# A fused attention and gated feed-forward kernel: the first combine spread over engines, one reciprocal moved to VectorE, two loads and stage 1 in later slots

## The chip, the core and the metric

The kernel runs on one core of a Trainium2 chip. A core has five engines with queues of their own: TensorE (PE; its weight loads are listed apart as PEld), VectorE (DVE), ScalarE (ACT), GpSimd (POOL) and SyncE (SP, which here only issues DMAs). Each engine works through its queue in order and waits on semaphores for the others. DMAs are issued from POOL (loads that cast from float32 to float16) and from SP (stores, and DMAs that transpose). The metric is the device time of one execution in microseconds (us).

## The reference

```python
def _attn_ref(x, inducing):            # x: 4 x 12416 x 128, inducing: 32 x 128
    def mab(q, kv):
        s = scale * (q @ kv.transpose(0, 2, 1))
        s = s - s.max(-1, keepdims=True)
        a = np.exp(s)
        a /= a.sum(-1, keepdims=True) + 1e-09
        return a @ kv
    h = mab(I, x)                      # stage 1: 32 inducing points attend to all x
    return mab(x, h)                   # stage 2: every x attends to the 32 rows of h

def _moe_ref(x, w_gate, w_val, w_out): # 128 -> 1536 -> 128
    gate = 1.0 / (1.0 + np.exp(-(x @ w_gate)))
    val = x @ w_val
    return gate * val @ w_out
```

The output is `_moe_ref` of the attention's result, for 4 x 12416 rows.

## The kernel before

**Tiles.** A batch is 97 chunks of 128 rows, in seven groups: six of 16 chunks and one of a single chunk (`groups`, L49). `xn[b]` holds the rows of a batch, `xT[b]` the same turned, both in float16 and two buffers each.

**Algebra.** Since stage 2 gives `a2 @ h`, the kernel first forms `hw = h @ w` for both weights (`hw_fill`, L289) and then multiplies the turned attention weights `a2` of 32 columns with it. So the hidden layer is 1536 columns in twelve parts, from a contraction over 32.

**Batch 0's stage 1** (L500 to L613) runs ahead of everything else, group after group as x arrives. Each group leaves a negated maximum (`nml`, `nm1`), a sum of exponentials (`l1l`) and a partial sum (`hst`, `hp`). The *first combine* (L546 to L613) merges them: `ml` is the maximum in each of 128 lanes (DVE, L560); `quad` and `top` bring the four lane groups of 32 onto one common maximum (POOL, four copies in, two minima, four copies out, L565 to L580); `w4` rescales the lanes (ACT, L582); `e32w` and `e32l` are the lane-folding matrix times w4 and times w4 and the sum (ACT, L584 and L599); `hpart` gathers the partial sums (DVE, four operations at L601); two matmuls, `l_ps` and `h_ps` (L610, L612), and a reciprocal give `hT`. POOL also issues the loads of the three weights, `wg` (L538), `wv` (L541) and `wo` (L544), and after `top` the first three loads of batch 1 (L586).

**The first group's stage 2** (L616 to L653) takes four chunks by PE turns, so that the main loop can begin (scores, maximum, exponential, sum, reciprocal, the spread `a2n` in four copies, turn, `a2first`), and the other twelve by DMA turns.

**The main loop** (L816 to L824) goes through 776 steps. A block is 4 chunks of 128 rows by twelve parts of the hidden layer, eight steps of two and one parts in turn. For step t, `product(t)` issues the value matmuls and one DVE operation (`u`, L699); `gate(t + 2)` the gate matmuls of the step after next and one ACT Tanh (`t`, L693); then, in even steps, `beside(t // 2)` issues the side work of one *slot*, and in odd ones `project` the matmuls into `acc` (L715), and at a block's end an ACT copy (`o`, L727) and a store. A slot is thus two steps; a group of 16 chunks lasts `SG` = 16 slots, a batch 96.

**The side work** is written as generators with a due slot (L737 to L759). `beside` first issues the loads that are due (`"x"`: a load on POOL, `"t"`: the DMA turn of x on SP), then advances each generator to its next `yield`. One PSUM tag, "m", is shared: a generator that says "take" waits until no other holds it, and it is free again a slot after "give".

- `stage2(b, c, n)` (L467), due 20 slots ahead of its group: scores in two slots, the maximum (DVE, L372) with `hi` and `lo` (POOL), two slots on the exponential (ACT, L394), then the sum as a tree on POOL (L402, L408), two slots on the reciprocal by four POOL operations (`s2_inverse_pool`, L423: `near`, `off`, `off`, `rs`) and the spread `a2n` (POOL, L448), two slots on the DMA turn (SP, L459) into `a2r`, which the matmuls of L678 read. `s2_inverse` (L418) is the same as one DVE reciprocal, used in the first group.
- `stage1(b + 1, g)` (L247), due at slot 5 + 6 g: scores and `nm` (DVE, L189), exponential (ACT, L202), DMA turn (SP, L226), six slots later the sum (PE, L235; ACT copy, L245).
- `combine(b + 1)` (L302) after them, then stage 2 of the next batch's first group.

Within one slot, generators go in the order of a small number: stage 2 first, then combine, then stage 1.

Of the kernel before, what the change touches and what calls it, by code (L numbers as in the profile page):

```python
# [9 lines left out]
F32 = mybir.dt.float32  # L10
# [3 lines left out]
ALU = mybir.AluOpType  # L14
AX = mybir.AxisListType

P = 128
GC = 16
BC = 4
NEG = 1.0e30  # L20
S1_LAG = 6
S2_LEAD = 20
COMBINE_LAG = 6

# [2 lines left out]
def kernel(  # L27
# [9 lines left out]
    nc = tc.nc  # L37
    B, N, C = x.shape
    m = inducing.shape[0]
# [48 lines left out]
    def x_transpose_dma(b, s):  # L88
# [16 lines left out]
        out=identf[:],  # L105
# [105 lines left out]
    def s1_turn_pe(b, s, a1T, tag="m"):  # L211
        ng, w, R = s1_dims(s)
        aT = ps.tile([P, 4, P], F16, tag=tag, name="aT_ps")
        for k in range(w):
            nc.tensor.transpose(aT[:, k, 0:R], a1T[0:R, ts(k, P)], ident[0:R, 0:R])
        return aT

    def s1_turn_copy(s, aT):
        ng, w, R = s1_dims(s)
        a1 = s1p.tile([P, 4, P], F16, tag="a1")  # L220
        nc.vector.tensor_copy(out=a1[:, 0:w, 0:R], in_=aT[:, 0:w, 0:R])
        return a1
# [6 lines left out]
    def s1_sum(b, s, a1, tag):  # L229
        c0, n = groups[s]  # L230
        ng, w, R = s1_dims(s)
        hp = ps.tile([P, C], F32, tag=tag, name="hp_ps")
        for k in range(w):
            for g in range(ng):
                nc.tensor.matmul(  # L235
                    hp[32 * g : 32 * g + 32, :],
                    a1[:, k, 32 * g : 32 * g + 32],
                    xn[b][:, c0 + g * w + k, :],
                    start=(k == 0),
                    stop=(k == w - 1),  # L240
                )
        summed[b] += 1
        if b == 0 and at_col[s] > EARLY:
            return hp
        nc.scalar.copy(out=hsts[b % 2][0:R, at_col[s], :], in_=hp[0:R, :])  # L245
# [177 lines left out]
    def s2_inverse_pool(n, sme):  # L423
        rs = s2p.tile([P, GC], F32, tag="rs")
        near = s2p.tile([P, GC], F32, tag="near")
        nc.gpsimd.tensor_tensor(  # L426
            out=near[:, 0:n], in0=sme[:, 0:n], in1=minus1[:, 0:n], op=ALU.pow
        )
        off = s2p.tile([P, GC], F32, tag="off")
        nc.gpsimd.tensor_tensor(  # L430
            out=off[:, 0:n], in0=sme[:, 0:n], in1=near[:, 0:n], op=ALU.mult
        )
        nc.gpsimd.tensor_scalar(
            out=off[:, 0:n],
            in0=off[:, 0:n],
            scalar1=-1.0,
            scalar2=2.0,
            op0=ALU.mult,
            op1=ALU.add,
        )  # L440
        nc.gpsimd.tensor_tensor(
            out=rs[:, 0:n], in0=near[:, 0:n], in1=off[:, 0:n], op=ALU.mult
        )
        return rs[:, 0:n]

    def s2_spread(n, e, rs, eng):
        a2n = s2p.tile([P, GC, 4, m], F16, tag="a2n")
        eng.tensor_tensor(  # L448
            out=a2n[:, 0:n, :, :],
            in0=e.unsqueeze(2).to_broadcast((P, n, 4, m)),  # L450
            in1=rs.unsqueeze(2).unsqueeze(3).to_broadcast((P, n, 4, m)),
            op=ALU.mult,
        )
        return a2n
# [9 lines left out]
        for j in range(n):  # L464
            a2[(b, c + j)] = (a2r, j)

    def stage2(b, c, n):  # L467
        yield "take"
        s2 = ps.tile([P, GC, m], F32, tag="m", name="s2_ps")
        half = (n + 1) // 2  # L470
        s2_score(b, c, 0, half, s2)
        yield
        s2_score(b, c, half, n, s2)
        hi, lo = s2_max(n, s2)
        yield
        yield
        e = s2_exp(n, s2, hi, lo)
        yield "give"
        sme = s2_sum_pool(n, e)
        yield  # L480
        yield
        rs = s2_inverse_pool(n, sme)
        a2n = s2_spread(n, e[:, 0:n, :], rs, nc.gpsimd)
        yield
        yield
        s2_turn_dma(b, c, n, a2n, "a2r" if n == GC else "a2l")
# [15 lines left out]
    for p in range(-2, NS - 3):  # L502
        if p + 2 < NS - 1:
            x_turn(0, *groups[arrival[p + 2]], ("g2", "v2")[p % 2])
        if p + 1 >= 0:
            s = arrival[p + 1]
            a1T[s] = s1_exp(0, s, s1_score(0, s, ("g1", "v1")[(p + 1) % 2]))
        if p >= 0:
            s = arrival[p]
            a1[s] = s1_turn_copy(s, s1_turn_pe(0, s, a1T[s]))  # L510
        if p - 1 >= 0:
            s = arrival[p - 1]
            s1_sum(0, s, a1[s], "acc")
        if p + 1 == EARLY - 1:

            we = const.tile([P, EARLY], F32, tag="we")
            nc.vector.tensor_reduce(
                out=nml[:, 0:1], in_=nm1[:, 0:EARLY], axis=AX.X, op=ALU.min
            )
            nc.scalar.activation(  # L520
                out=we[:], in_=nm1[:, 0:EARLY], func=AF.Exp, bias=nml[:, 0:1], scale=-1.0
            )
            lw = const.tile([P, EARLY], F32, tag="lwe")
            nc.gpsimd.tensor_tensor(out=lw[:], in0=l1[:, 0:EARLY], in1=we[:], op=ALU.mult)
            add_tree(lw, EARLY, l1l[:, 0:1])
            hpart = [const.tile([P, C], F32, name=f"hpart{k}", tag=f"hpart{k}") for k in range(2)]

            def pool_part(p):
                nc.gpsimd.tensor_scalar_mul(
                    out=hpart[p > 0][:], in0=hst[:, p, :], scalar1=we[:, p : p + 1]  # L530
                )
                if p > 0:
                    nc.gpsimd.tensor_tensor(
                        out=hpart[0][:], in0=hpart[0][:], in1=hpart[1][:], op=ALU.add
                    )

            pool_part(0)
            nc.gpsimd.dma_start(wg16[:], moe_w_gate.rearrange("c (i t f) -> c i t f", t=2, f=P))  # L538
        elif p == EARLY - 1:
            pool_part(1)  # L540
            nc.gpsimd.dma_start(wv16[:], moe_w_val.rearrange("c (i t f) -> c i t f", t=2, f=P))  # L541
        elif p == EARLY:
            pool_part(2)
            nc.gpsimd.dma_start(wo16[:], moe_w_out.rearrange("(j p) c -> p j c", p=P))  # L544

    sc, sb, sa = arrival[-1], arrival[-2], arrival[-3]  # L546
    c0, n = groups[sc]
# [29 lines left out]
    )  # L577
    top = const.tile([P, 1], F32, tag="top")
    for g in range(4):
        nc.gpsimd.tensor_copy(out=top[32 * g : 32 * g + 32, :], in_=quad[:, 0:1])  # L580
    w4 = const.tile([P, 1], F32, tag="w4")
    nc.scalar.activation(out=w4[:], in_=ml[:], func=AF.Exp, bias=top[:], scale=-1.0)  # L582
    e32w = const.tile([P, m], F32, tag="e32w")
# [4 lines left out]
    a1[sa] = s1_turn_copy(sa, aT)  # L588
    a1[sb] = s1_turn_copy(sb, s1_turn_pe(0, sb, a1T[sb], "g2"))
    hps = [hst[:, EARLY, :], s1_sum(0, sa, a1[sa], "acc")[:]]  # L590
    a1[sc] = s1_turn_copy(sc, s1_turn_pe(0, sc, a1T[sc], "v2"))
    hps.append(s1_sum(0, sb, a1[sb], "m")[:])
    hps.append(s1_sum(0, sc, a1[sc], "v1")[:])
    lw = const.tile([P, 1 + NS - EARLY], F32, tag="lwl")
    nc.vector.tensor_mul(out=lw[:], in0=l1l[:], in1=wl[:])
    lsum = const.tile([P, 1], F32, tag="lsum0")
    nc.vector.reduce_sum(out=lsum[:], in_=lw[:], axis=AX.X)
    e32l = const.tile([P, m], F32, tag="e32l0")
    nc.scalar.mul(out=e32l[:], in_=e32w[:], mul=lsum[:])  # L599
    for k, hp in enumerate(hps):  # L600
        nc.vector.scalar_tensor_tensor(  # L601
            out=hpart[0][:],
            in0=hp,
            scalar=wl[:, 1 + k : 2 + k],
            in1=hpart[0][:],
            op0=ALU.mult,
            op1=ALU.add,
        )
    l_ps = ps.tile([P, m], F32, tag="g1", name="l_ps")
    nc.tensor.matmul(l_ps[:], ones[:], e32l[:], start=True, stop=True)  # L610
    h_ps = ps.tile([P, m], F32, tag="m", name="h_ps")
# [23 lines left out]
    hw_ps = [hw_fill(0, 0, "g1"), hw_fill(0, 1, "v1")]  # L635
    for hf in range(2):
        nc.scalar.copy(out=hw[0][:, ts(hf, NI // 2), :], in_=hw_ps[hf][:])
    a2n_a = s2_spread(BC, e_a[:], s2_inverse(BC, s2_sum_dve(BC, e_a)), nc.vector)
    e_b = s2_exp(GC - BC, s2_b, *hl_b)
    a2T = ps.tile([P, BC, P], F16, tag="m", name="a2T_ps")  # L640
    for j in range(BC):
        nc.tensor.transpose(
            a2T[:, j, :], a2n_a[:, j, :, :].rearrange("p r k -> p (r k)"), ident[:]
        )
    a2first = s2p.tile([P, BC, P], F16, tag="a2first", bufs=1)
    nc.vector.tensor_copy(out=a2first[:], in_=a2T[:])
# [94 lines left out]
    for b in range(B):  # L741
        at = base[b]
        for s in range(1, NS):
            c, n = groups[s]
            lead = S2_LEAD if s < NG else S2_LEAD + SG // 2
            work.append((max(0, at + SG * s - lead), 0, lambda b=b, c=c, n=n: stage2(b, c, n)))
        if b + 1 < B:
            for g in range(NS):
                loads.append((at + (5 if b == 0 else 3) * g, "t", b + 1, g))
                if b == 0 and 3 <= g < NG:  # L750
                    loads.append((at + 5 * g - 12, "x", 1, g))
                work.append((at + 5 + 6 * g, 2, lambda b=b, g=g: stage1(b + 1, g)))
            work.append((at + 5 + 6 * NS, 1, lambda b=b: combine(b + 1)))
            work.append((at + SG * NG - S2_LEAD, 0, lambda b=b: stage2(b + 1, NLO, GC)))
        if b + 2 < B:
            for g in range(NG):
                loads.append((at + 24 + 9 * g, "x", b + 2, g))
# [98 lines left out]
```

## Time and profile before

| | |
|---|---|
| median of 3 runs | 770.66 us (770.39 to 771.56) |
| the profiled execution | 771.34 us, span 769.6 us |
| busy: DVE, ACT, PE, POOL | 735.9, 672.6, 671.3, 279.8 us |
| mean granted TensorE clock | 0.984 |
| DMA | 65.16 MB, mean 85 GB/s |
| DVE u (L699), 776 instructions | 692.0 us |
| ACT t (L693), 776 instructions | 598.6 us |
| DMA turns a2r<-a2n (L459), 29, issue to landing | 2.3 / 4.9 / 12.8 us (least, median, most) |

All times within the span count from its start. A row of a timeline gives the start, the busy time, engine and line, what is written from what, the shapes, and in brackets how long the engine was idle before it and what ended that. Rows of the same kind that follow one another are merged, with a count. The chain of waits is the sequence of work that ended last, followed back from the end; "issue" in it is time in which the engine waited for nothing that the profile shows. A clock of 0.50 is half the full TensorE clock.

### The profile page before, as it was taken

How to read it: one execution, taken by the hardware profiler on the slowest of the kernel's cores; microseconds unless marked ns; L12 is line 12 of the kernel's file. 1: busy time of each engine (PE TensorE's matmuls, PEld its weight loads, DVE VectorE, ACT ScalarE, POOL GpSimd, SP SyncE). 2: the span in 40 equal slices, each digit the busy share in tenths (PEclk: the TensorE clock that was granted, in tenths of full speed). 3: DMA queues.
4: the chain of work that ended last, by engine and by line, in shares of the span. 5: the costliest groups of instructions: out<-in, count | busy, mean ns of one | idle time of the engine just before them, and what ended most of it. 6: DMA issues, size and time to landing. Idle time of an engine off the chain costs nothing.

```text
span 769.6 us, 20801 instructions
## 1 busy us (share of the span) xinstructions
PE 671.3 (87%) x8167; PEld 403.5 (52%) x8167; DVE 735.9 (96%) x908; ACT 672.6 (87%) x1007; POOL 279.8 (36%) x445
## 2 busy tenths in 40 slices
PE   6788889899888898989888889988988888988887
PEld 4354555555555455555555455555555555555554
DVE  3798999999999999999999999999999999999997
ACT  4687989889989999989989899988989899899996
POOL 3551450472440523545504224246235135045100
PEclk9688999999999999999999999999999999999999
DMA  8979735424239255174056632121121220230311
GB/s 167 152 129 189 139 62 107 98 55 99 71 83 165 66 109 122 36 117 99 29 97 133 117 84 63 49 57 51 49 70 35 64 69 31 69 69 29 72 43 43
DMA packets 117730, 65.16 MB, mean 85 GB/s; under 512 B 101344, under 2 KB 102016, under 8 KB 117632
## 3 DMA queue, kind: packets, MB, share of 16 engines
q1 hardware_dynamic: 112192, 49.94, 28.2%
q0 software_dynamic: 5440, 13.90, 11.5%
q8 instruction: 64, 1.05, 0.6%
q14 instruction: 34, 0.28, 0.1%
HBM read 27.80 MB, written 25.43 MB: 69 GB/s over the span
## 4 chain that ended last, share of the span: by engine, by line
DVE 37%; PE 25%; issue 20%; ACT 13%; DMA 2%; POOL 2%; ACTq 0%; DVEq 0%; POOLq 0%
DVE u L699 33%; PE acc_ps L715 10%; PE v_ps L678 10%; ACT t L693 10%; PE s_ps L361 2%; DMA a2r<-a2n 2%; DVE nmx L372 2%; PE g_ps L678 1%; ACT e L394 1%; DVE nm L189 1%; ACT a1T L202 1%; PE xt_ps L493 1%; DMA xn<-in_x_dram 1%; PE s_ps L385 0%; POOL a2n L448 0%
## 5 line engine op out<-in xcount | busy, mean ns | idle before, releaser
L699 DVE SCALAR_TENSOR_TENSOR u<-t,v_ps 128x1024 f16<-128x1024 f16 (+1 forms) x776 | 692.0, 948 | 12.8 <-PE g_ps L678 4.7
L693 ACT ACTIVATE t<-g_ps 128x1024 f16<-128x1024 f32 (+1 forms) x776 | 598.6, 819 | 69.7 <-PE g_ps L678 53.9
L678 PE MATMUL v_ps<-a2r,hwt 32*128 32x512 f16 (+1 forms) x1188 | 293.8, 372 | 77.8 <-DVE u L699 73.6
L715 PE MATMUL acc_ps<-wo,u 128*128 128x128 f16 x4656 | 329.8, 221 | 0.9
L715 PEld LDWEIGHTS <-u 128*128 128x128 f16 x4656 | 263.7, 98 | 98.6 <-issue 97.1
L678 PE MATMUL g_ps<-a2r,hwt 32*128 32x512 f16 (+1 forms) x1188 | 296.6, 379 | 1.9 <-DMA a2r<-a2n 1.2
L678 PEld LDWEIGHTS <-hwt 32*128 32x128 f16 x2400 | 99.8, 91 | 214.2 <-issue 166.2
L376 POOL CAST hi<-nmx 128x16 bf16<-128x16 f32 (+2 forms) x28 | 5.5, 195 | 279.6 <-DVE nmx L372 279.5
L448 POOL TENSOR_TENSOR a2n<-e,rs 128x2048 f16<-128x2048 f16 (+2 forms) x28 | 86.9, 3105 | 5.0 <-PE g_ps L678 2.9
L426 POOL TENSOR_TENSOR near<-sme,minus 128x16 f32<-128x16 f32 (+1 forms) x27 | 69.7, 2583 | 2.1
L727 ACT ACTIVATE o<-acc_ps 128x512 f32<-128x512 f32 x97 | 58.8, 607 | 4.6 <-PE acc_ps L715 4.6
L402 POOL TENSOR_TENSOR sum<-e 128x256 f32<-128x256 f16 (+1 forms) x27 | 16.1, 598 | 88.2 <-ACT e L394 88.2
L402 POOL TENSOR_TENSOR sum<-sum 128x128 f32<-128x128 f32 (+3 forms) x108 | 31.5, 292 | 8.5
L361 PEld LDWEIGHTS <-xT 128*128 128x128 f16 x388 | 13.7, 97 | 12.8 <-issue 12.5
L361 PE MATMUL s_ps<-hT,xT 128*128 128x32 f16 x388 | 18.2, 179 | 0.9 <-DVE hT L287 0.5
L372 DVE TENSOR_REDUCE nmx<-s_ps 128x16 f32<-128x512 f32 (+2 forms) x28 | 17.0, 606 | 0.8 <-PE s_ps L361 0.8
L202 ACT ACTIVATE a1T<-s_ps,nm 128x512 f16<-128x512 f32 (+1 forms) x24 | 15.1, 630 | 1.7 <-DVE nm L189 1.7
L189 DVE TENSOR_REDUCE nm<-s_ps 128x1 f32<-128x512 f32 (+1 forms) x24 | 14.7, 614 | 0.9 <-PE s_ps L177 0.9
L82 POOL DMA_DIRECT2D xn<-in_x_dram x25 | 15.1, 612 | 0.9 <-POOLq L840 0.8
L394 ACT ACTIVATE e<-s_ps 128x512 f16<-128x512 f32 (+2 forms) x28 | 14.9, 533 | 0.6 <-PE s_ps L385 0.6
L497 ACT COPY xT<-xt_ps 128x1024 f16<-128x1024 f16 (+1 forms) x6 | 5.6, 939 | 8.5 <-PE xt_ps L493 8.5
L495 DVE COPY xT<-xt_ps 128x1024 f16<-128x1024 f16 (+2 forms) x8 | 4.7, 598 | 8.7 <-PE xt_ps L493 8.7
(104 smaller groups left out, 200.6 us busy)
## 6 DMA issues: line engine op xcount, KB each, us to landing
out_dram<-o SPq DMA_DIRECT2D x97, 256.0 KB, 2.4
xn<-in_x_dram POOLq DMA_DIRECT2D x19, 512.0 KB, 6.9
xn<-in_x_dram POOLq DMA_DIRECT2D x4, 544.0 KB, 6.0
a2r<-a2n SPq DMA_TRANSPOSE x29, 4.9
xn<-in_x_dram POOLq DMA_DIRECT2D x1, 384.0 KB, 14.3
wg<-in_moe_w_gate_dram POOLq DMA_DIRECT2D x1, 384.0 KB, 4.5
wv<-in_moe_w_val_dram POOLq DMA_DIRECT2D x1, 384.0 KB, 6.4
wo<-in_moe_w_out_dram POOLq DMA_DIRECT2D x1, 384.0 KB, 6.6
```

The lines of the kernel that those rows point to most:

```text
L202: nc.scalar.activation(out=a1T[0:R, 0 : w * P], in_=s1[0:R, 0 : w * P], func=AF.Exp, bias=nm[0:R, col], accum_out=l1[0:R, col],)
L361: nc.tensor.matmul(s2[:, j, :], xT[b][:, c + j, :], hT16[b][:], start=(j == 0), stop=whole and j == j1 - 1, skip_group_check=True,)
L372: nc.vector.tensor_reduce(out=nmx[:, 0:n], in_=s2[:, 0:n, :], axis=AX.X, op=ALU.max, negate=True)
L394: nc.scalar.activation(out=e[:, 0:n, :], in_=s2[:, 0:n, :], func=AF.Exp, scale=SCALE)
L402: nc.gpsimd.tensor_tensor(out=d[:, 0:n, :], in0=src[:, :, 0:w], in1=src[:, :, w : 2 * w], op=ALU.add)
L426: nc.gpsimd.tensor_tensor(out=near[:, 0:n], in0=sme[:, 0:n], in1=minus1[:, 0:n], op=ALU.pow)
L448: eng.tensor_tensor(out=a2n[:, 0:n, :, :], in0=e.unsqueeze(2).to_broadcast((P, n, 4, m)), in1=rs.unsqueeze(2).unsqueeze(3).to_broadcast((P ...
L678: nc.tensor.matmul(pt[:, k, col : col + nb * P], hw[b][r : r + 32, j // 2, :], a2r[r : r + 32, o : o + nb, :].rearrange("p j t -> p (j t)" ...
L693: nc.scalar.activation(out=st["t"][:], in_=st["g"][:], func=AF.Tanh, scale=0.5)
L699: nc.vector.scalar_tensor_tensor(out=st["u"][:], in0=st["t"][:], scalar=1.0, in1=st["v"][:], op0=ALU.add, op1=ALU.mult)
L715: nc.tensor.matmul(acc[0][:, i, :], st["u"][:, k, ts(i, P)], wo16[:, j, :], start=(j == 0 and i == 0), stop=(j == NJ - 1), skip_group_chec ...
L727: nc.scalar.mul(out=o32[:], in_=acc[0][:], mul=0.5)
```

## The change

Five things are altered.

1. In the first combine, the load of `wo` moves from ahead of `quad` to behind `top`, still on POOL. Two of the four copies of `top` go to ACT. `lw` and `lsum` move ahead of the last copy of stage 1, and `e32l` is one DVE operation (e32 times w4 times lsum) between the third and the fourth operation of L601, where it was an ACT multiply of `e32w` by `lsum`.
2. In the first group's stage 2 the spread of four chunks is two spreads of two chunks.
3. For group 1 of batch 0 the reciprocal is `s2_inverse` (DVE) where it was `s2_inverse_pool`.
4. The loads of groups 3, 4 and 5 of batch 1 are due in slots 3, 14 and 17, where they were due in slots 3, 8 and 13.
5. Stage 1 of batches 1 to 3, and the combine behind it, are due two slots later (`S1_FIRST` = 7 for 5).

```diff
+S1_FIRST = 7
...
-    def stage2(b, c, n):
+    def stage2(b, c, n, soon=False):
...
-        rs = s2_inverse_pool(n, sme)
+        rs = (s2_inverse if soon else s2_inverse_pool)(n, sme)
...
             pool_part(2)
-            nc.gpsimd.dma_start(wo16[:], moe_w_out.rearrange("(j p) c -> p j c", p=P))
...
     for g in range(4):
-        nc.gpsimd.tensor_copy(out=top[32 * g : 32 * g + 32, :], in_=quad[:, 0:1])
+        if g % 2:
+            nc.scalar.copy(out=top[32 * g : 32 * g + 32, :], in_=quad[:, 0:1])
+        else:
+            nc.gpsimd.tensor_copy(out=top[32 * g : 32 * g + 32, :], in_=quad[:, 0:1])
+    nc.gpsimd.dma_start(wo16[:], moe_w_out.rearrange("(j p) c -> p j c", p=P))
...
     hps = [hst[:, EARLY, :], s1_sum(0, sa, a1[sa], "acc")[:]]
-    a1[sc] = s1_turn_copy(sc, s1_turn_pe(0, sc, a1T[sc], "v2"))
-    hps.append(s1_sum(0, sb, a1[sb], "m")[:])
-    hps.append(s1_sum(0, sc, a1[sc], "v1")[:])
     lw = const.tile([P, 1 + NS - EARLY], F32, tag="lwl")
     nc.vector.tensor_mul(out=lw[:], in0=l1l[:], in1=wl[:])
     lsum = const.tile([P, 1], F32, tag="lsum0")
     nc.vector.reduce_sum(out=lsum[:], in_=lw[:], axis=AX.X)
-    e32l = const.tile([P, m], F32, tag="e32l0")
-    nc.scalar.mul(out=e32l[:], in_=e32w[:], mul=lsum[:])
+    a1[sc] = s1_turn_copy(sc, s1_turn_pe(0, sc, a1T[sc], "v2"))
+    hps.append(s1_sum(0, sb, a1[sb], "m")[:])
+    hps.append(s1_sum(0, sc, a1[sc], "v1")[:])
     for k, hp in enumerate(hps):
...
+        if k == len(hps) - 2:
+            e32l = const.tile([P, m], F32, tag="e32l0")
+            nc.vector.tensor_scalar(
+                out=e32l[:],
+                in0=e32[:],
+                scalar1=w4[:],
+                scalar2=lsum[:],
+                op0=ALU.mult,
+                op1=ALU.mult,
+            )
...
-    a2n_a = s2_spread(BC, e_a[:], s2_inverse(BC, s2_sum_dve(BC, e_a)), nc.vector)
+    rs_a = s2_inverse(BC, s2_sum_dve(BC, e_a))
+    a2n_a = [
+        s2_spread(BC // 2, e_a[:, j : j + BC // 2, :], rs_a[:, j : j + BC // 2], nc.vector)
+        for j in range(0, BC, BC // 2)
+    ]
...
+            soon = b == 0 and s == 1
...
                 if b == 0 and 3 <= g < NG:
-                    loads.append((at + 5 * g - 12, "x", 1, g))
-                work.append((at + 5 + 6 * g, 2, lambda b=b, g=g: stage1(b + 1, g)))
-            work.append((at + 5 + 6 * NS, 1, lambda b=b: combine(b + 1)))
+                    loads.append((at + (3, 14, 17)[g - 3], "x", 1, g))
+                work.append((at + S1_FIRST + 6 * g, 2, lambda b=b, g=g: stage1(b + 1, g)))
+            work.append((at + S1_FIRST + 6 * NS, 1, lambda b=b: combine(b + 1)))
```

## Prediction

> **What bounds the kernel now.** I read the page first: its busy shares, its forty slices (19.24 us each) and the clock row.
>
> ```profile
> PE 671.3 (87%) x8167; PEld 403.5 (52%) x8167; DVE 735.9 (96%) x908; ACT 672.6 (87%) x1007; POOL 279.8 (36%) x445
> ...
> DVE  3798999999999999999999999999999999999997
> ...
> PEclk9688999999999999999999999999999999999999
> ```
>
> From the fifth slice on, VectorE (DVE) is full, so there only work taken off DVE would pay, and nothing here is. What can be won lies in slices two to four: there DVE is below 9 at times and the granted TensorE clock is not full. So I cut those slices into stages (columns: stage, its length, busy us of PE, PEld, DVE, ACT, POOL, then clock, DMA share, GB/s).
>
> ```profile
> 65.00:68.00 3.00, 1.80 (x22) 0.81 (x19) 1.93 (x3) 1.16 (x3) 0.00 (x0) 0.85 1.19 295
> 68.00:70.00 2.00, 2.00 (x18) 1.33 (x18) 1.12 (x2) 0.96 (x2) 0.41 (x2) 0.50 1.02 250
> 70.00:72.00 2.00, 2.00 (x22) 1.24 (x16) 1.68 (x2) 1.51 (x2) 0.00 (x0) 0.50 1.09 197
> 72.00:74.00 2.00, 2.00 (x10) 0.32 (x10) 1.36 (x2) 1.94 (x3) 0.00 (x0) 0.52 0.80 165
> ```
>
> From 65 to 68 all engines run short at once; then, to 73.9, the clock is 0.50, PE is full and DVE starves. The DVE timeline prices it: the number in brackets is the idle time before the row.
>
> ```profile
> 65.82 1.22 DVE L699 SCALAR_TENSOR_TENSOR u<-t,v_ps 128x1024 f16<-128x1024 f16 x1 [0.27 <-ACT t L693]
> 67.84 0.69 DVE L372 TENSOR_REDUCE nmx<-s_ps 128x16 f32<-128x512 f32 x1 [0.80 <-PE s_ps L361]
> 68.45 0.68 DVE L699 SCALAR_TENSOR_TENSOR u<-t,v_ps 128x512 f16<-128x512 f16 x1
> 70.32 1.82 DVE L699 SCALAR_TENSOR_TENSOR u<-t,v_ps 128x1024 f16<-128x1024 f16 x2 [1.19 <-PE g_ps L678]
> 72.68 1.22 DVE L699 SCALAR_TENSOR_TENSOR u<-t,v_ps 128x1024 f16<-128x1024 f16 x1 [0.54 <-ACT o L727]
> 74.16 0.69 DVE L699 SCALAR_TENSOR_TENSOR u<-t,v_ps 128x512 f16<-128x512 f16 x1 [0.26 <-PE g_ps L678]
> 75.27 3.00 DVE L699 SCALAR_TENSOR_TENSOR u<-t,v_ps 128x1024 f16<-128x1024 f16 x3 [0.42 <-PE g_ps L678]
> ```
>
> 0.80 + 1.19 + 0.54 + 0.26 + 0.42 = 3.21 us lost. The 0.27 ahead of them also stands at 84.99 and 92.95, so it is ordinary. The same timeline, with all engines, names the cause.
>
> ```profile
> 46.47 2.95 POOL L426 TENSOR_TENSOR near<-sme,minus 128x16 f32<-128x16 f32 x1
> ...
> 50.40 3.61 POOL L448 TENSOR_TENSOR a2n<-e,rs 128x2048 f16<-128x2048 f16 x1
> ...
> 53.95 1.19 POOL L82 DMA_DIRECT2D xn<-in_x_dram  x2
> ...
> 54.04 6.65 SPq L459 DMA_TRANSPOSE a2r<-a2n  x1
> ...
> 66.92 0.49 PE L678 MATMUL g_ps<-a2r,hwt 32*128 32x512 f16 x2 [1.20 <-DMA a2r<-a2n]
> ```
>
> Two loads of batch 1 start just ahead of the turn of group 1. Last, the chain of waits, before and in that place:
>
> ```profile
> 22.62 1.07 POOL wo L544
> ...
> 26.31 1.13 issue
> 27.44 0.62 PE l_ps L610 x2
> ...
> 54.04 12.83 DMA a2r<-a2n
> ```
>
> So the turn takes 12.83 us, and the first combine's chain runs through the issue of the load of wo.
>
> **The loads (L751).** By the views of DMA issues, turns of 16 chunks with no load beside them (203.19, 232.27) land in 4.8 and 4.6 us; with one load issued just before (84.46, 113.34, 143.27, 173.14) in 7.6, 9.1, 8.9, 7.6 (10.1 at 324.43); with two in 12.8. POOL runs its queue without waiting between slots 8 and 13, so "slot 8" and "slot 13" both meant 53.95. I wrote the slots out by hand from L737 on. In the new order the loads stand behind the hi and lo of group 2 (slot 13; L376 waits for DVE's nmx) and behind its sums (slot 16). Group 2 itself moves from slots 14-22 to 12-20, because group 1 of stage 1 no longer holds the PSUM tag "m" at slot 12. The loads then issue near 62 and 70 us. The turn of group 1 has none beside it: 54.0 + 4.8 = 58.8, against 65.72 (66.92 - 1.20), when PE wants it. The wait goes with 6.9 us to spare, and next late is DVE itself.
>
> What the loads meet instead: the turns of x (groups 4 and 5, slots 20 and 25) need them; issued near 62 and 70, landing in 7 to 10 us, they are there by about 72 and 80, while slot 20 comes near 73 and slot 25 near 82 (a slot is about 1.9 us; they fall 3 us sooner without the stall). On SP the turn of x group 4 stands ahead of group 2's a2n turn, which is not ready before 77 (sum near 66.3, 10.1 us of POOL as between 74.25 and 84.37, and 0.62 for the second load, now in that chain). It lands in 7.6 near 85; group 2 is wanted near 98. Cover 13 us. The two issues of 0.6 us on POOL only move. Take: -3.2 us; bounds -0.8 (only the wait) and -3.5.
>
> **One reciprocal on DVE (L482).** It removes four POOL operations (2.95 + 0.22 + 0.21 + 0.22, 46.47 to 50.32) and adds one on DVE. That one stands in slot 6, behind u of step 12. With steps of 0.60 and 1.17 (seven in 5.95) step 12 ends at 48.20 + 0.60 + 1.17 = 49.97; without the nm of 0.60 that the shift takes out of slot 5, at 49.37. Reciprocals of 128x4 and 128x12 take 0.18 and 0.23, so about 0.24 for 128x16: rs at 49.6 instead of 50.32. The turn starts 0.7 sooner, not 3.9. Its operand sme is there at 46.39, so DVE doesn't wait; behind it u of step 13 is 0.24 later. With the wait gone by the loads alone, those 0.7 buy nothing: +0.2.
>
> **The first combine (L542 to L616).** POOL: hpart ends at 22.62, wo takes until 23.69, quad starts at 23.70. But ml ends on DVE only at 23.48, so taking wo out gains 23.70 - 23.53 = 0.17, not 1.07. Four top copies take 25.48 to 26.31; two on POOL and, beside them, two on ACT (idle there for 1.50 us) end near 25.72 + 0.1 - 0.17: ACT's price isn't shown for this shape, between READ_ACCUMULATOR's 0.19 and the Exp of 128x1's 0.29; I take 0.24, its copy of 32x128. Tops end at 25.7, w4 at 26.0 instead of 26.63. Then e32l: before, two ACT multiplies of 0.32 in a row ended at 27.34. Now it is one DVE operation behind the third L601. lw and lsum (0.15, 0.16) go into DVE's 0.31 of idle before the last copy, so the third L601 ends near 26.3 and e32l (0.19 as L280 of the same size, at most 0.35 as L601) near 26.5; the last L601 ends near 26.9, as before. l_ps starts at 26.6 instead of 27.44, and h_ps at 27.0 instead of 27.86: -0.8. The spread in halves costs two operations of some 0.38 for one of 0.69, but the last two of four turns on PE start behind it (0.62 for four): -0.05. wo lands 3 us later, near 32.5, and is first used at 37.77. All that follows shifts by 0.85, but PE runs at 0.50 until 43.2, and there DVE is idle 2.0 of the 8.6 us from 34.6. If the clock rises at the same moment, 0.85 us more work is done slow: +0.2. Take -0.65; bounds 0 and -1.3.
>
> **Stage 1 two slots later.** No instruction more or less. DVE's idle in full slices is 0.15 of 30 us without stage 1 and 0.3 to 0.7 with it (ACT's a1T beside o), about 1.2 per batch. Other slots give another meeting of the two: 0, bounds -1 and +1.
>
> **Sum.** -3.2 + 0.2 - 0.65 + 0 = -3.65. The profiled execution took 771.34 (span 769.6, 1.74 around it): 767.7. The median of the runs is 770.66, 0.68 below the profiled one: **767.0**.
>
> **Rivals.**
> *The clock falls anyway.* Then only the 0.80 of wait goes: -0.65 - 0.8 + 0.2 = -1.25, 769.4. For it: PE was idle 0.99 us at 22.5, and 4.0 us for the first x, and the clock stayed at 1.00, so 1.20 us of idle need not be the cause at 67.1. Against: the record shows two falls (26.2 and 67.1), each in or right behind a long idle time of PE (1.91 and 1.20), and full clock from 73.9 to the end, where no idle is over 1.0. 7 in 100. Beside it: the Trainium skill, "TensorE: Matmul & The Clock Gate", section "HAM oscillation", has the rule "no PE-idle gaps >~3.4µs", by which a gap of 1.20 would not throttle and this change would keep the slow stretch. Here the clock fell within 0.2 us of its end, which speaks against the rule in that form.
>
> *The first turns meet the loads.* wo moved behind the tops can push loads 0 to 2 back by 1.5 us, beside the turn of block 1 (34.55 + 5.1 = 39.65, wanted at 41.52). Its 1.9 us of cover could go; up to 1.5 lost: 768.5. DMA is full through that stretch either way. 8 in 100.
>
> *Slower: group 4 comes late.* In batches 0 to 2 stage 2 of group 4 moves from slot 44 to 46 (the DMA slot from 52 to 54), because stage 1 now holds "m" at 44. Its a2n ends near 143.2 + 3.8 + 0.6 = 147.6, and PE wants it at 160.9. A landing over 13.3 us decides. In batch 1 it took 10.1 with one load, and two gave 12.8. In the two batches that also load (0 and 1), each stall costs the 3.2 us above: -3.65 + 6.4 = +2.75, 773.4. Against: the load of slot 51 now issues ahead of near, 7 us before the turn. 6 in 100.
>
> *It doesn't do what it says*: the turn stays at 12.8 for another reason. The wait is then still 0.7 shorter (0.5 of 1.2 is left) and the clock decides: -0.65 - 0.5 + 0.2, 769.7. 5 in 100.
>
> **How the numbers follow.** Forecast 74 in 100, its own range 765.2 to 768.8 (bounds of the combine and of stage 1, not all at one end). The range reaches up to 769.5 to take in the clock rival. About 0.2% (1.5 us) is what a measurement can tell from no change, so faster is below 769.1: 0.74 + 0.08 = 0.82, same 0.07 + 0.05 = 0.12, slower 0.06.
>
> **What would show it.** The turn of group 1 lands in about 5 us near 57; no PE wait for a2r; clock 1.00 from 43 on; DVE full from 62 to 78; l_ps 0.8 sooner; reciprocal near 48.8, straight behind u. Wrong would be a fall of the clock without that wait, or a new PE wait for a2r at block 1 or in group 4.

## The result and the profile after

The changed kernel's median is **768.34 us** (767.20 to 769.34 in 22 runs); the kernel before, run on the same occasions, 770.15 (767.81 to 772.63 in 22 runs). The ratio is 0.9978 with an interval of 0.9969 to 0.9987: 0.22% faster, and the medians lie 1.81 us apart. The forecast was 767.0 with a range of 765.2 to 769.5, so the time is in the range and the sign is right, but about half of the 3.65 us came. The profiled execution took 768.34 (span 766.5, mean granted clock 0.989).

The page shows the shares, and in the forty slices DVE and the clock:

```profile
PE 669.1 (87%) x8167; PEld 402.6 (53%) x8167; DVE 736.3 (96%) x911; ACT 672.4 (88%) x1008; POOL 275.7 (36%) x439
...
DVE  4889999999999999999999999999999999999997
...
PEclk9689999999999999999999999999999999999999
```

The fourth digits of DVE and of the clock, both 8 before, are now 9. The second and third, the stretch before and in the first steps of the loop, are still below. The stages where the stall had been (the columns are as in the prediction):

```profile
65.00:68.00 3.00, 3.00 (x41) 1.79 (x41) 2.85 (x4) 3.00 (x5) 1.46 (x4) 1.00 0.99 152
68.00:70.00 2.00, 1.20 (x16) 0.68 (x16) 2.00 (x3) 1.98 (x4) 1.74 (x5) 1.00 0.50 140
70.00:72.00 2.00, 1.80 (x24) 1.07 (x22) 2.00 (x4) 1.44 (x3) 2.00 (x1) 1.00 1.01 124
72.00:74.00 2.00, 1.95 (x36) 1.26 (x34) 2.00 (x4) 2.00 (x6) 1.67 (x5) 1.00 0.95 162
```

DVE is busy 8.85 of the 9 us and the clock is 1.00. What made it so stands in the timeline (SPq is SP's DMA queue, so 1.86 is the time it took to issue):

```profile
48.44 0.24 DVE L421 RECIPROCAL rs<-sme 128x16 f32<-128x16 f32 x1
...
48.77 3.61 POOL L449 TENSOR_TENSOR a2n<-e,rs 128x2048 f16<-128x2048 f16 x1 [3.48 <-DVE rs L421]
...
52.40 1.86 SPq L460 DMA_TRANSPOSE a2r<-a2n  x1
...
63.02 0.62 POOL L83 DMA_DIRECT2D xn<-in_x_dram  x1
```

The two loads that stood at 53.95 now issue at 63.02 and 68.90. The turn of group 1 has none beside it and lands 5.7 us after its issue, where it took 12.8. No PE wait for `a2r` is left.

The first combine after:

```profile
23.11 0.84 POOL L566 COPY quad<-ml 32x1 f32<-32x1 f32 x4 [0.92 <-DVE ml L560]
...
24.84 0.39 ACT L581 COPY top<-quad 32x1 f32<-32x1 f32 x2 [0.44 <-POOL quad L575]
24.87 0.39 POOL L583 COPY top<-quad 32x1 f32<-32x1 f32 x2
...
25.21 1.15 POOL L584 DMA_DIRECT2D wo<-in_moe_w_out_dram  x1
...
25.72 0.61 DVE L613 TENSOR_SCALAR e32l<-e,w,lsum 128x32 f32<-128x32 f32 x1
...
26.48 0.60 PE L622 MATMUL l_ps<-e32l,ones 128*128 128x32 f32 x2 [1.32 <-DVE hpart L603]
```

POOL now waits for `ml`, the tops run side by side, and from the end of `ml` to `l_ps` it takes 3.43 us (23.05 to 26.48), where it took 3.96 (23.48 to 27.44): 0.53 sooner. But `wo` is issued 2.6 us later than it was, and in the stage from 24 to 28 us that shows:

```profile
24.00:28.00 4.00, 1.95 (x40) 1.42 (x38) 2.89 (x11) 1.40 (x5) 3.73 (x8) 0.68 0.47 64
28.00:32.00 4.00, 3.00 (x34) 1.30 (x35) 3.02 (x11) 1.55 (x4) 0.41 (x2) 0.50 1.35 193
```

Before, the first of these stages was:

```profile
24.00:28.00 4.00, 1.91 (x55) 1.37 (x47) 2.30 (x8) 1.68 (x7) 3.47 (x12) 0.76 1.29 147
```

The DMA engines moved 64 GB/s from 24 to 28 us (share 0.47), where it was 147 (share 1.29): with `wo` issued late, they had less than half as much to do in this stretch.

### The profile page after: what moved, and what is told of

Its sections match the earlier page's. It is cut to its first block, busy times and chain, and to the rows that moved or that the text cites. A ratio compares the mean times of both kernels' runs of the same rounds, so it can differ in the third digit from the quotient of the medians.

```text
span 766.5 us, 20798 instructions
## 1 busy us (share of the span) xinstructions
PE 669.1 (87%) x8167; PEld 402.6 (53%) x8167; DVE 736.3 (96%) x911; ACT 672.4 (88%) x1008; POOL 275.7 (36%) x439
## 4 chain that ended last, share of the span: by engine, by line
DVE 34%; PE 28%; issue 20%; ACT 14%; POOL 4%; DMA 1%; ACTq 0%; DVEq 0%; POOLq 0%
DVE u L717 30%; PE acc_ps L733 11%; PE v_ps L696 11%; ACT t L711 10%; PE s_ps L362 2%; DVE nm L190 2%; DVE nmx L373 2%; ACT a1T L203 1%; PE g_ps L696 1%; ACT e L395 1%; ACT o L745 1%; PE xt_ps L494 1%; POOL near L427 1%; PE s_ps L386 1%; DMA xn<-in_x_dram 1%
## 5 line engine op out<-in xcount | busy, mean ns | idle before, releaser
L427 POOL TENSOR_TENSOR near<-sme,minus 128x16 f32<-128x16 f32 (+1 forms) x26 | 66.9, 2572 | 1.9
L395 ACT ACTIVATE e<-s_ps 128x512 f16<-128x512 f32 (+2 forms) x28 | 14.9, 533 | 0.6 <-PE s_ps L386 0.6
```

What stands on the lines that cost most here:

```text
L427: nc.gpsimd.tensor_tensor(out=near[:, 0:n], in0=sme[:, 0:n], in1=minus1[:, 0:n], op=ALU.pow)
```

## The experiments

**Theories.** A: the stall of group 1 was the price, the loads take it away, and the rest gives little. B: the late `wo` makes its own stall, and the shift of stage 1 covers it. C: the clock's falls, not the waits themselves, carry the time, and they come and go from one execution to the next. The kernel before ran beside each. Medians in us:

| run | edit | median | before, same chip | ratio (interval) |
|---|---|---|---|---|
| e1_loads_only | before, with the loads moved | 768.20 | 770.78 | 0.9975 (0.9961 to 0.9988) |
| e2_front_only | parts 1 and 2 alone | 770.83 | 770.78 | 1.0013 (0.9997 to 1.0030) |
| e3_loads_back | after, loads back | 768.75 | 770.78 | 0.9981 (0.9965 to 0.9997) |
| e4_shift_only | before, with stage 1 shifted | 772.57 | 770.78 | 1.0033 (1.0017 to 1.0049) |
| e5_shift_back | after, without the shift | 767.60 | 769.73 | 0.9978 (0.9963 to 0.9993) |
| e6_front_and_loads | parts 1, 2, 4, `wo` early | 769.01 | 769.73 | 0.9995 (0.9983 to 1.0007) |
| e7, e8 (before again) | none, one execution each | 767.99, 768.50 | 769.73 | |
| e9_warm | after, 15 idle matmuls | 773.92 | 770.17 | 1.0033 (1.0010 to 1.0057) |
| e10_after_again | none (5 runs) | 767.76 | 770.17 | 0.9964 (0.9952 to 0.9977) |
| e11_wo_first | after, `wo` early | 767.88 | 770.76 | 0.9967 (0.9956 to 0.9979) |
| e12_warm_wo_first | e11, 17 idle matmuls | 768.92 | 770.76 | 0.9999 (0.9970 to 1.0028) |

**e1_loads_only.**

```diff
-                    loads.append((at + 5 * g - 12, "x", 1, g))
+                    loads.append((at + (3, 14, 17)[g - 3], "x", 1, g))
```

> The kernel before with the loads of batch 1 due in slots 3, 14 and 17 and nothing else changed. Here stage 2 of group 2 still starts in slot 14, so the load of slot 14 stands ahead of its hi and lo on POOL and still issues straight behind group 1's spread; only the load of slot 17 goes away from the turn. Theory A (the prediction: the wait and the slow stretch cost 3.2 us in every execution): the turn of group 1 lands in 7.6 to 10.1 us as other turns with one load, no PE wait, no second fall of the clock, 3.2 us less than before, 767.0 beside a before of 770.15. Theory B (the clock falls behind the wait only in some executions, because its window runs free of the kernel, so the wait is worth 0.8 in some and 3.2 in others; the 22 times of before lie in two heaps, 767.8 to 769.0 and 769.8 to 772.6): the profile the same, but the median only 1 to 2 us below before, near 768.6, and all times in one heap.

The turn lands in 8.6 us with the one load still beside it (53.93; the other moved to 68.36), no PE wait for `a2r` is left, and the clock doesn't fall again. This one line gives the whole measured gain.

**e2_front_only.** After, with the loop as before:

```diff
-S1_FIRST = 7
+S1_FIRST = 5
...
-            soon = b == 0 and s == 1
+            soon = False
...
-                    loads.append((at + (3, 14, 17)[g - 3], "x", 1, g))
+                    loads.append((at + 5 * g - 12, "x", 1, g))
```

> The first combine and the halved spread of the changed kernel, with the loop's side work as before (reciprocal on POOL, loads in slots 8 and 13, stage 1 from slot 5). Theory A: 0.65 us less than before, 769.5 beside 770.15; the wait for group 1's turn and the fall of the clock remain, l_ps about 0.5 us sooner against what arrives ahead of it. Theory B: the same shift in the profile, and times in two heaps as before's, so that the median may move by up to 2 us either way with the share of each heap. A rival for the missing gain, that the combine gains nothing because PE's slow stretch takes it back, would give 0.

The profiled execution was slower than any of the kernel before on that chip (773.59). Its PE has a wait that the profile of before does not have:

```profile
48.80 0.62 PE L178 MATMUL s_ps<-xT,indT 128*32 128x512 f16 x4 [3.71 <-DMA xT<-xn]
```

The turn of batch 1's first group landed 11.4 us after its issue at 37.31 (6.7 before), 3.7 us after stage 1 in slot 5 wanted it, and from 47.4 to 54.2 the clock was 0.50. This fits theory B, that the first loads of batch 1 meet this turn: the last of the three landed 3.0 us after the turn was issued, where it was 1.3 in the profile of before. That the late `wo` alone makes the wait is not shown (see e8).

**e3_loads_back.** After, with the line of e1 undone.

> The changed kernel with the two loads due in slots 8 and 13 again. The turn starts 0.7 us sooner against the loop than before (reciprocal on DVE), so with a landing of 12.8 us a PE wait of about 0.5 us remains of 1.2. Theory A: wait 0.5 and a fall of the clock with 2.4 us: 2.9 us slower than the changed kernel, 771.2 beside 768.34. Theory B: a wait of 0.5 us in every execution and the fall in some: 0.5 to 2 us slower, two heaps. If the loads did not matter, it would equal the changed kernel.

The turn of group 1 took 11.6 us with both loads beside it, but nobody waited. Counted from the first `u` it is issued after 18.8 us (52.41 less 33.64), where before it was 19.4 (54.04 less 34.62). Its 11.6 us are also less than the 12.8 in the profile of before. So of the 1.9 us by which the landing came sooner, 0.65 is the earlier issue, to which reciprocal and shift both belong, and 1.2 is a length that differs between executions of one kernel (10.9 to 12.8 in before). By the median the rest of the change covers most of what the loads cover; which part of it does is not shown. Ten of the 12 runs lie between 767.45 and 769.25, two at 770.87 and 772.18.

**e4_shift_only.** Before, with `at + 5 + 6 * ...` made `at + 7 + 6 * ...` for stage 1 and the combine.

> The kernel before with stage 1 and the combine of later batches two slots later and nothing else changed. Theory A: without effect on the wait (the nm of 0.6 us leaves DVE ahead of it, but the reciprocal on POOL and the loads stay), the rest 0 with bounds of 1 either way. Rival C for the gain that is missing: the shift costs 1 us or more in the three batches, since the changed kernel's profile falls back by 1.5 us against before's behind step 48; then 1 to 1.5 us slower than before, 771.2 to 771.7 beside 770.15.

All 12 runs took 771.35 or more (to 776.04). The wait for `a2r` (landing 12.0) is still there, and with it a fall of the clock from 66.3 on; another comes at 158.5:

```profile
65.76 0.39 PE L678 MATMUL g_ps<-a2r,hwt 32*128 32x512 f16 x2 [0.73 <-DMA a2r<-a2n]
```

PE is ready for group 1 at 65.03 (65.76 less 0.73), 30.7 us after the first `u` at 34.32; before it was 31.1 (65.72 less 34.62). So the shift alone brings the loop to the turn 0.4 us sooner while the turn starts as it did. (In e3 the landing, 30.4 us after the first `u`, makes that limit by 0.3.) Why every run is so long stays open: three of them have a mean clock of 0.988 or more and still took 771.4 to 771.8, so a fall of the clock is not the whole reason.

**e5_shift_back.** After, with `S1_FIRST = 5`.

> The changed kernel with stage 1 due from slot 5 again, the rest as changed. Theory (from the front-only kernel, where stage 1's first score waited 3.7 us for the turn of x group 0 behind loads that wo had pushed back): the shift is what covers that turn, which landed 9.3 us after its issue at 36.53 in the changed kernel, at 45.8, where slot 5 wants it near 45. So a PE wait of 0.5 to 4 us at the score of slot 5, a fall of the clock, and 770 to 772. Rival: the shift covers nothing and only costs some 0.5 us later on; then 767.8, half a us below the changed kernel.

The wait for `xT` came, as e2 had shown, at less than half the length, and the clock didn't fall there:

```profile
46.82 0.40 PE L178 MATMUL s_ps<-xT,indT 128*32 128x512 f16 x4 [1.61 <-DMA xT<-xn]
```

The price expected of it did not come: the ratio is that of the full change. So by the medians the shift gains nothing and costs nothing, though it hides this wait.

**e6_front_and_loads.** After, with `S1_FIRST = 5`, `soon = False`, and the load of `wo` back ahead of `quad`.

> The kernel before with the late loads and the first combine's new order, but with the load of wo where it was, the reciprocal on POOL and stage 1 from slot 5. Theory: wo ahead of quad costs 0.17 us of the combine, the loads keep the wait away, nothing pushes the turn of x group 0 back and no shift or reciprocal costs anything: 0.5 us below the loads alone (768.2) and the changed kernel (768.34), 767.7. Rival (the combine's gain is eaten by the slow stretch up to 43): 768.2.

No wait for `xT` (its turn took 6.3 us) and none for `a2r`. Yet 769.01 instead of the sum expected: the clock fell at 330.2 for one stretch of 3.4 us, in the profiled execution, behind the `col` of the main loop's second combine (DVE, L315, at 328.11), where PE is idle for 0.96:

```profile
328.00:330.00 2.00, 1.03 (x11) 0.33 (x9) 1.93 (x7) 1.14 (x3) 0.53 (x3) 1.00 0.00 0
330.00:332.00 2.00, 2.00 (x25) 1.37 (x24) 1.35 (x3) 1.08 (x3) 1.81 (x4) 0.56 0.00 0
```

PE is half idle in the first line, runs at about half speed in the second, and DVE is idle for 0.65 us there and for 0.62 a little later (before the `u` at 334.36). Such single falls also stand in the profiles of e4, e5, e9 and e12, always 2 to 4 us behind the first of four `col`. The fall is not the whole reason for 769.01: the three runs with a mean clock of 0.988 or more took 767.2, 769.1 and 770.1. The rest stays open.

**e7_before_again, e8_before_again2, e10_after_again.** The two kernels unchanged, profiled once more, for theory C.

> The kernel before, to see another execution of it. Its 35 times on the last chip lie in heaps at 766.8 to 769.4 and 770.0 to 772.2. Theory: the turn of group 1 lands 11.5 to 13 us after its issue, and PE wants it after 11.7; where it lands in time there is neither wait nor fall of the clock, and the execution takes some 768, as with the loads moved; where it is late, wait and fall, some 771. Rival: wait in both heaps, and only the clock differs.

> The kernel before once more, for the same two theories: a time near 768 with no wait for group 1's turn, or a time near 771 with a wait and a fall of the clock; or, by the rival, a wait with either time.

> The changed kernel once more, beside the one with extra matmuls on one chip. Theory: no wait for the turn of group 1 or of x group 0 in any execution; what is left of its spread comes from the length of the slow stretch (13.7 or 17.1 us) and from single falls of the clock behind a batch's combine, as the kernels before have shown at 158.5, 330.3 and 513.2: 767.2 to 769.4, median 768.3, some 2 us below the kernel before.

In e7 the turn took 12.8 us, as in the profile of before, and PE waited longer for it (1.61 for 1.20). But the clock did not fall (1.00 from 41.1 to 764.7). PE and DVE in that place:

```profile
65.97 0.39 PE L678 MATMUL g_ps<-a2r,hwt 32*128 32x512 f16 x2 [1.61 <-DMA a2r<-a2n]
```

```profile
66.76 0.69 DVE L372 TENSOR_REDUCE nmx<-s_ps 128x16 f32<-128x512 f32 x1 [1.08 <-PE s_ps L361]
67.37 7.55 DVE L699 SCALAR_TENSOR_TENSOR u<-t,v_ps 128x512 f16<-128x512 f16 x8
```

A wait of 1.61 with a full clock costs DVE 1.08 us, and eight `u` follow without a gap. The wait of 1.20 with the fall had cost 3.21. What differs is how the wait lies to the stretches of 3.41 us in which the clock changes (the last section says how they are found). In before, the whole wait lies in one, with PE busy for 2.12 of 3.42 us, and the clock fell at its end; in e7 it is divided over two, with PE busy for 2.64 and 2.42:

```profile
63.66:67.08 3.42, 2.12 (x26) 1.20 (x25) 3.12 (x4) 1.95 (x4) 0.00 (x0) 1.00 1.14 240
```

```profile
61.58:64.99 3.41, 2.64 (x34) 1.49 (x30) 3.14 (x5) 2.66 (x6) 0.00 (x0) 1.00 1.10 181
64.99:68.41 3.42, 2.42 (x30) 1.32 (x30) 2.20 (x4) 1.77 (x3) 0.41 (x2) 1.00 1.18 292
```

In e8 the turn took 10.9 us and there was no wait for `a2r` at all; instead PE waited 1.7 us for `xT`, whose turn took 9.6 us, and the clock fell for 3.4 us behind that. So the unchanged kernel has this wait too, in some executions; the late `wo` is not needed for it. In e10 the changed kernel again has no wait (turn 5.9 us) and no second fall, and its slow stretch at the front is 13.7 us long instead of 17.1.

**e9_warm.** After, with 15 matmuls whose results nobody reads, where PE is idle in the front (5 ahead of `l_ps`, then 3, 3, 2, and 2 in the loop's first steps):

```diff
+    def fill(count, tag, banks):
+        warm = ps.tile([P, banks, 512], F32, tag=tag, name="warm_ps")
+        for k in range(count):
+            nc.tensor.matmul(warm[:, k % banks, :], ident[:], xT[0][:, 4 * k : 4 * k + 4, :]...)
...
+    fill(5, "g2", 2)
```

> The changed kernel with 15 matmuls more that nobody reads (128x128 by 512, into PSUM that is free there), put where PE idles in the first combine and the first group's stage 2: 5 ahead of l_ps, 3 ahead of the first scores, 3 ahead of the exponential's, 2 behind the four turns, 2 behind the first product. Theory (the clock follows PE's activity in windows of 3.41 us: in all profiles so far it falls between 23.1 and 28.7 us, while PE idles, and stays at 0.50 for 13.7 or 17.1 us): the fall doesn't come or comes late and short; PE is at full clock by the first block, DVE's 2.0 us of idle between 34 and 43 go, and the small matmuls of the chain get shorter: 1 to 2.5 us below the changed kernel, near 766.5. Rival (the clock of that stretch is not set by PE's idle time): the same 13.7 to 17.1 us at 0.50, the extra matmuls cost up to 1 us, 768.3 to 769.3.

The fills did hold the clock (1.00 until 34.4, then 0.50 for 6.8 us instead of 17.1), and the main loop began at 32.76 instead of 33.52. But in 24 to 28 the DMA engines moved only 26 GB/s, and the turn of x took 18.6 us:

```profile
54.79 0.62 PE L178 MATMUL s_ps<-xT,indT 128*32 128x512 f16 x4 [6.72 <-DMA xT<-xn]
```

**e11_wo_first.** After, with one line put back:

```diff
         elif p == EARLY:
             pool_part(2)
+            nc.gpsimd.dma_start(wo16[:], moe_w_out.rearrange("(j p) c -> p j c", p=P))
```

> The changed kernel with the load of wo ahead of quad again, the rest as changed. Theory: behind the tops, wo left the DMA engines half empty from 24 to 28 us (64 GB/s where the kernel before moved 147) and pushed loads 0 to 2 of batch 1 against the first turns, so that the turn of x group 0 took 9.3 and 9.9 us instead of 6.7. Ahead of quad it costs the combine at most 0.2 us and the turn lands in 6 to 8.5 us, well ahead of slot 7: within 0.3 us of the changed kernel, 768. Rival (wo's place gains the 1.07 us that stood in the chain of waits): 0.8 slower or more.

The DMA engines move 147 GB/s in 24 to 28 again, the turn of x takes 7.9 us, and the issue of `wo` costs the combine nothing: from the end of `ml` to `l_ps` it is 3.12 us, 0.3 shorter than in after, since `e32l` takes 0.29 us. First `u` at 32.75. Its median lies 2.9 us below its own before, 1.8 (and 2.4 in e10) for the change itself; the intervals overlap.

**e12_warm_wo_first.** e11 with 17 fills.

> The same with 17 matmuls more that nobody reads, in PE's idle time (5 ahead of l_ps, 3 ahead of the first scores, 3 ahead of the exponential's, 2 behind the four turns, 4 behind the first product). With 15 of them and wo behind the tops the clock stayed at 1.00 until 34.3 and the loop began 0.75 us sooner, but the turn of x group 0 took 18.6 us and slot 7 waited 6.7. Theory (that wait came from wo's place): with wo first it lands in 6 to 9 us, no wait, and the gain of the clock stays: 1 to 2 us below the kernel of the other run, 766.5. Rival (the extra matmuls themselves bring the collision, by starting the turns sooner): the wait stays at 3 us or more, 770 to 774.

In the profiled execution (766.45) the clock is 1.00 from the start to 152.8; the same stages as shown for after, and the next:

```profile
28.00:32.00 4.00, 3.73 (x40) 1.42 (x39) 3.25 (x11) 1.57 (x5) 0.41 (x2) 1.00 1.05 211
32.00:36.00 4.00, 3.72 (x40) 1.84 (x40) 3.93 (x7) 4.00 (x6) 2.31 (x1) 1.00 1.06 198
```

Six runs lie at 765.26 to 766.53, the lowest of any kernel here among them, six at 771.30 to 775.68. The first six have a mean clock of 0.997 to 0.999, the others 0.991 to 0.995, so these do have one to three stretches more at half clock. But after has runs at 0.991 too, with times of 767.2 to 768.4, so half clock somewhere does not explain 771 or more. No profile of such a run exists, and the cause stays open; a wait for `xT` as in e9 would fit.

## Why the prediction was half right

Every execution comes with its mean granted clock, and for the kernel before that sorts them. With 3.41 us at half clock worth 0.002 of the mean, 0.988 or more is five such stretches or fewer (the slow start of the loop is four or five); less is one or two more. It is a rough measure: a start of four with one fall counts like a start of five, and most records also have some half clock in the last microsecond or two, when PE has nothing left to do (e8, at 0.987, has 2.2 us of that).

| | runs | clock 0.988 or more | median of these | clock below | median of these |
|---|---|---|---|---|---|
| before, beside e1 to e12 | 98 | 23 | 768.0 | 75 | 770.8 |
| e1_loads_only | 12 | 11 | 768.2 | 1 | 768.2 |
| after | 22 | 21 | 768.3 | 1 | 768.8 |
| e2_front_only | 12 | 4 | 769.9 | 8 | 771.9 |
| e11_wo_first | 12 | 10 | 767.4 | 2 | 768.5 |

It does not sort every kernel: the three runs of e4 at 0.988 or more have a median of 771.7, the three of e6 769.1, the ten of e9 773.2.

**The loads: mechanism right, size too big.** The step was "-3.2; bounds -0.8 (only the wait) and -3.5". e1 gives 2.6 by the medians and 1.9 by the ratio. The term came from one execution, in which the wait met a fall of the clock. By this measure, before falls a second time in about three executions of four, and where it doesn't, it is already as fast as after. e7 and e8 show why: a landing of 10.9 to 12.8 us stands right at the limit (about 11.7), so the wait comes or not, and where it comes, its place in the 3.41 us stretches decides whether the fall comes with it. A stall that isn't always there is worth its mean: 0.75 of about 2.8 (770.8 less 768.0) is 2.1. The profiled 771.34 was of the heavier kind, which the 0.68 taken off the median didn't make good.

**The reciprocal: close.** 0.24 us at 48.44, straight behind `u`, and the turn starts sooner after the first `u` by 0.5 us (18.88 for 19.42; 0.7 in e10), where the prediction had 0.7. It costs its 0.24 and can be worth something only as margin; no run has it alone.

**The first combine: right size, wrong cover.** "-0.8" for `l_ps` was 0.53, and e11 gives 0.84 (3.96 less 3.12): the missing 0.3 is `e32l`, "0.19, at most 0.35", which takes 0.61 where POOL issues `wo` beside it and 0.29 in e11, where it issues the loads of x. (In e6, with the same order but the clock at 0.50 from 23.0 on, `e32l` takes 0.41 and the stretch 3.58.) To the first `u`, the stretch from the end of `ml` is 0.7 us shorter in after (10.47 for 11.15), as forecast, but the runs show no gain of it: e2 equals before, and after equals e1.

The step that failed is "DMA is full through that stretch either way": with `wo` late the DMA engines move less than half as much there, and the three loads land no sooner (the last 15.4 us behind `ml` in after, 15.5 before, 14.9 in e11), while the loop that needs the engines begins sooner. The rival that named this had the wrong victim. The turn of block 1 has no wait; that of x for stage 1 can have one: its length follows how far the loads overlap it. It took 4.4 us where the last load had landed before the issue (e1), 6.3 to 9.6 where it landed 0.0 to 2.0 us behind it (before, e4, e6 to e8, e11, e12, and after), and 9.7 to 11.4, in e9 18.6, where it was 2.5 to 3.0 (e2, e3, e5, e9, e10). In after the shift hides the wait. The prediction had not seen that, so this was luck.

**The shift: not told apart from 0.** From the first `u` to the last, after takes 727.68 us, e10, the same kernel, 727.17, and e1 726.95. So two executions of one kernel differ by 0.5, and beyond the reciprocal's 0.24 nothing can be put down to the shift. e4 points to a cost (1.8 us above its before), e5 to none (2.1 below its before, without the shift). Of the missing 1.8 us of the forecast, about 1.1 is the loads' term (3.2 for 2.1); the rest is the front's 0.65, which the runs do not show, and where it goes stays open. After stands where e1 stands (768.3 and 768.2 in the table).

**The rivals.** The clock did not fall anyway: in after, e1, e10 and e11 it is full from the front's slow stretch on. Group 4 was not late. The turn of group 1 did not stay at 12.8. The mark set for "wrong", a fall without that wait, was met by other kernels, behind `col`, not by after.

## What to carry to other kernels

A stall seen in one profile has a price only once it is known how often it is there: profile the same kernel two or three times, and sort the timed executions by their mean clock, before its idle times go into a sum. A load that is issued later is not free because the DMA engines are "full": look at what the queue holds in the time it leaves, and which later transfer pays. Two edits can cover the same stall, and one can cover what the other breaks; only runs of each alone show it, and here the reciprocal never ran alone.

## What the hardware showed

The granted clock is 0.50 for 3.4, 6.8, 10.2, 13.7 or 17.1 us, multiples of 3.41, in every trace here (the last stretch, which the end of the record cuts off, apart). The Trainium skill, "TensorE: Matmul & The Clock Gate", section "What's actually happening", has a free-running window of 3413 ns; the lengths agree with it. The stretches at 1.00 in between are multiples too (23.89 us from 43.18 to 67.08 in before, 7 times 3.41), so all changes of the clock in a trace lie on one grid (within 2 ns), and each trace shows where its windows begin.

Counted in these windows, PE's busy time (by the profile, which models the ends of matmuls) tells where the clock falls. Between 40 and 750 us the 14 traces have 2897 windows at full clock. In 2880 of them PE was busy for 70% or more, and the clock fell behind none. In five it was busy for 62% or less, and the clock fell behind each; of the twelve in between it fell behind five. So the place of the windows against the kernel, which differs in each execution, accounts for a wait of 1.20 us that brought a fall (62% busy) and one of 1.61 that did not (77% and 71%). The same page's section "HAM oscillation" has the rule against idle gaps over about 3.4 us; as a limit it does not hold here, where falls stand behind single gaps of 0.96 and 1.20 us. Nor does 0.96 us always bring one: each of the seven profiles without the shift has three such gaps, and of these 21 two had a fall behind them.

Keeping PE busy with 17 unread matmuls held the clock at 1.00 through the whole front (e12), and a better front did not make a steadier kernel. The same turn by DMA (group 1) took 4.5 to 5.9 us alone, 7.8 to 9.1 with one load beside it and 10.9 to 12.8 with two, without any change to it.
